# Transposing queries and keys of groups 1 to 3 by DMA instead of by TensorE, in sigmoid attention followed by an MLP mixer

## The chip, the cores and the metric

The kernel runs on one core of a Trainium2 chip. A core has TensorE (PE; its weight loads are shown as PEld), VectorE (DVE), ScalarE (ACT), GpSimd (POOL) and SyncE (SP), which each work through a queue of their own in order and wait for one another by semaphores, and 16 DMA engines, which serve the transfers that SP and POOL issue. The metric is the device time of one execution in microseconds (us); lower is better. Names such as `tk_1_2591` are the program's tiles; the last number is a running number of the buffer.

## What is computed

Eight batches, twelve heads, sequence 448, head dimension 64. Attention with a sigmoid in place of the softmax, then a mixer over tokens and one over channels:

```python
scores = scale * np.matmul(q, k.transpose(0, 1, 3, 2)) - np.log(S)
attn = 1.0 / (1.0 + np.exp(-scores))
attn_out = np.matmul(attn, v)                      # (8, 12, 448, 64)
x = attn_out.transpose(0, 2, 1, 3).reshape(B, S, H * D)   # (8, 448, 768)
xt = x.transpose(0, 2, 1)
h = np.maximum(xt @ w_tok1, 0.0) @ w_tok2          # 448 -> 256 -> 448 over tokens
u = x + h.transpose(0, 2, 1)
h2 = np.maximum(u @ w_ch1, 0.0) @ w_ch2            # 768 -> 1536 -> 768 over channels
return u + h2
```

## The kernel before

The batches go in four groups g of two (`b`), and the twelve heads of a group in six pairs i. A token is numbered 7p + j (p below 64, j below 7), so that the 128 partitions of a tile hold the 64 p of both batches, and j runs along the free dimension.

*Loading* (`load`, L75 and L83). The queries and keys of a pair come as float32 tiles `rawq`, `rawk` by two DMAs each on the SP queue, and are cast to float16 tiles `q`, `k` of [128, J, 2, 64], by VectorE for the very first pair and by GpSimd for all others. The values `v` are cast by the DMA itself, on POOL's queue. There are four raw buffers, three of `q` and three of `k`, six of `v`: a load waits for a cast to have read its raw buffer, a cast for its `q` or `k` buffer to be read.

*A pair of attention* (`attention_atoms`). `turn(i)` transposes `k` and `q` to have the head dimension on the partitions: for each of the two, seven 128x128 transposes on TensorE (L131), one for each j, into a PSUM bank, and a VectorE copy to `kT` (L135) or `qT` (L137); the copy of `qT` also reorders it so that a batch's 448 tokens lie together. `scores(i, j)` makes a tile of scores `qk` by four matmuls of 64x448 (L147), and ScalarE's sigmoid turns it to `attn` (L154). `values(i)` multiplies by `v` (L168), `back(i)` transposes the result to `x_nat` (L187, L190).

*The mixer of a group* (`mixer_atoms`). `tok1` (L222) and ScalarE's relu (L230) make `h1T`; `tok2` (L240) is added to `x_nat` by VectorE to give `u` (L247), cast (L252) and transposed (`uturn`, L257 and L262) to `uT`; `ch1` (L267, L274) makes `h2aT`; `ch2` (L286, L294) adds to `u`, and SP stores it (L297), two DMAs for each j.

*Order.* TensorE's instructions stand in the order in which they are written (`manual_schedule`). Group 0's attention stands alone; after that, `weave` puts the attention of group g+1 between the pieces of group g's mixer by a table of weights; the last mixer stands alone. The other queues are ordered by the scheduler, from the instructions' dependences and buffers. Eight PSUM banks serve: two tiles of two banks for scores, and four single banks (`bank`) shared in turn by all else, the transposes too.

Of the kernel before, what the change touches and what calls it, by code (L numbers as in the profile page):

```python
# [9 lines left out]
FP16 = mybir.dt.float16  # L10
# [9 lines left out]
def kernel(  # L20
# [13 lines left out]
    nc = tc.nc  # L34
# [5 lines left out]
    J = 7  # L40
    P = S // J
# [12 lines left out]
    pa = ctx.enter_context(tc.tile_pool(name="pa", bufs=2))  # L54
# [10 lines left out]
    heads = {}  # L65
# [46 lines left out]
    def bank(name, shape, dtype=FP32):  # L112
        return pp.tile(shape, dtype, tag="m", bufs=4, name=name)
# [3 lines left out]
    def attention_atoms(g):  # L117

        qT, kT, attn, xT = {}, {}, {}, {}
        x_nat = pa.tile([128, J, D], FP16, tag="x_nat", bufs=2, name=f"x_nat_{g}")  # L120
        x_nats[g] = x_nat

        def turn(i):
            kt = pa.tile([128, J, 2, P], FP16, tag="kT", bufs=2, name=f"kT_{g}_{i}")
            qt = pa.tile([128, 2, J, P], FP16, tag="qT", bufs=2, name=f"qT_{g}_{i}")
            kT[i], qT[i] = kt, qt
            for what in ("k", "q"):
                ps = bank(f"t{what}_{g}_{i}", [128, J, 2, P], FP16)
                src = heads[(g, i, what)]
                for j in range(J):  # L130
                    nc.tensor.transpose(  # L131
                        out=ps[:, j, :, :], in_=src[:, j, :, :], identity=ident[:, :]
                    )
                if what == "k":
                    nc.vector.tensor_copy(out=kt[:, :, :, :], in_=ps[:, :, :, :])  # L135
                else:
                    nc.vector.tensor_copy(  # L137
                        out=qt.rearrange("e b j p -> e j b p"), in_=ps[:, :, :, :]
                    )

        def scores(i, j):
            ps = pp.tile([128, 2, 512], FP32, tag="qk", bufs=2, name=f"qk_{g}_{i}_{j}")
            at = pa.tile([128, 2, S], FP16, tag="attn", bufs=11, name=f"attn_{g}_{i}_{j}")
            attn[(i, j)] = at
            for b in range(2):
                for h in range(2):
                    nc.tensor.matmul(  # L147
                        out=ps[64 * b : 64 * b + 64, h, 0:S],
                        lhsT=kT[i][64 * h : 64 * h + 64, j, b, :],
                        rhs=qT[i][64 * h : 64 * h + 64, b, :, :],  # L150
                        start=True,
                        stop=True,
                    )
            nc.scalar.activation(  # L154
                out=at[:, :, :],
                in_=ps[:, :, 0:S],
                func=SIGMOID,
                bias=bias_t[:, :],
                scale=att_scale,
            )  # L160

        def values(i):
            ps = [bank(f"xa_{g}_{i}_{b}", [128, S]) for b in range(2)]
            vf = heads[(g, i, "v")]
            for j in range(J):
                for h in range(2):
                    for b in range(2):
                        nc.tensor.matmul(  # L168
                            out=ps[b][64 * h : 64 * h + 64, :],
                            lhsT=vf[64 * b : 64 * b + 64, h, j, :],  # L170
                            rhs=attn[(i, j)][64 * b : 64 * b + 64, h, :],
                            start=(j == 0),
                            stop=(j == J - 1),
                        )
            xt = pa.tile([128, J, 2, P], FP16, tag="xT", bufs=2, name=f"xT_{g}_{i}")
            xT[i] = xt
            for b in range(2):
                nc.scalar.activation(
                    out=xt[:, :, b, :],
                    in_=ps[b].rearrange("d (j p) -> d j p", j=J),  # L180
                    func=COPYF,
                )

        def back(i):
            ps = bank(f"xb_{g}_{i}", [128, J, 128], FP16)
            for j in range(J):
                nc.tensor.transpose(  # L187
                    out=ps[:, j, :], in_=xT[i][:, j, :, :], identity=ident[:, :]
                )
            nc.vector.tensor_copy(  # L190
                out=x_nat[:, :, 128 * i : 128 * i + 128], in_=ps[:, :, :]
            )

        atoms = []
        nv = NP * J // 2
        for n in range(nv):

            def visit(n=n):
                for r in (2 * n, 2 * n + 1):
                    scores(r // J, r % J)  # L200

            atoms.append((float(n), 0.45, visit))
        for i in range(NP):
            atoms.append((i * J / 2 - 1.4, 0.8, lambda i=i: turn(i)))
            last = (i * J + J - 1) // 2
            atoms.append((last + 1.01, 1.4, lambda i=i: values(i)))
            atoms.append((last + 1.9, 0.4, lambda i=i: back(i)))
        return sorted(atoms, key=lambda a: a[0])
# [183 lines left out]
```

## Time and profile before

| | us |
|---|---|
| three runs | 433.65, 439.6, 435.13 |
| their median | 435.13 |
| the profiled execution | 434.62 |
| its span, first to last instruction | 432.8 |
| mean granted TensorE clock | 0.994 |

The times of single instructions below come from the profiled execution alone, whose span is 1.8 us shorter than its time. Loading and group 0's attention take the first 67 us of it, with the DMA engines busy nearly throughout; the three woven stretches, each of some 97 us, follow; the last mixer begins near 362 us. A line of the time view gives start, length, engine, source line, operation, the tile written and the tiles read, and in brackets what ended the idle time before it. A line of the stretch view gives the stretch, its length, for PE, PEld, DVE, ACT and POOL the busy time (and instructions), the granted clock, the busy share of the DMA engines and their GB/s. A line of the DMA view ends with the size of each transfer and the median time from issue to landing.

### The profile page before, as it was taken

What the parts mean: (1) busy time and instruction counts of PE and PEld (TensorE: products, weight loads), DVE (VectorE), ACT (ScalarE), POOL (GpSimd) and SP (SyncE); (2) the same over time, 40 slices, a digit from 0 to 9 for tenths busy, and PEclk for the clock granted to TensorE, in tenths of its full rate; (3) what the DMA queues carried; (4) which work ended last, traced back from release to release, by engine and by line L of the source; (5) the groups of instructions that cost most, each with busy time, mean ns of one, the idle gap of its engine ahead of it and who ended that gap; (6) DMA issues with size and microseconds to landing.
All of it is one profiled execution on the core that took longest, in us unless ns stands there. A gap on an engine that the chain in (4) does not pass through costs nothing.

```text
span 432.8 us, 8713 instructions
## 1 busy us (share of the span) xinstructions
PE 396.2 (92%) x3712; PEld 215.7 (50%) x3712; DVE 174.8 (40%) x312; ACT 216.8 (50%) x277; POOL 74.5 (17%) x105
## 2 busy tenths in 40 slices
PE   1775668999999999999999999999999999999995
PEld 1343335444555555444565555444555555546663
DVE  2131213845542224844542224844542224855322
ACT  1768884774546643775546643765546643300000
POOL 3851516021221211021221211011000000000000
PEclk9999989999999999999999999999999999999999
DMA  8999999335237643234337643200002221000234
GB/s 202 246 261 248 259 266 216 85 87 108 60 69 180 161 92 69 77 88 105 67 63 180 163 93 73 71 2 2 2 2 74 73 74 38 2 0 2 54 94 109
DMA packets 28023, 44.51 MB, mean 103 GB/s; under 512 B 3280, under 2 KB 23504, under 8 KB 27984
## 3 DMA queue, kind: packets, MB, share of 16 engines
q1 hardware_dynamic: 18304, 33.04, 28.6%
q0 software_dynamic: 9680, 10.92, 15.4%
q8 instruction: 29, 0.48, 0.5%
q14 instruction: 10, 0.08, 0.1%
HBM read 43.84 MB, written 11.01 MB: 127 GB/s over the span
## 4 chain that ended last, share of the span: by engine, by line
PE 85%; ACT 7%; issue 3%; DVE 2%; DMA 1%; SPq 0%; ACTq 0%; DVEq 0%
DMA rawq_0_76<-in_q_dram 1%; PE xa_5_0_787 L168 1%; PE xa_0_0_273 L168 1%; PE c_2_5_1_4890 L286 0%; PE c_2_4_1_4846 L286 0%; PE c_2_4_0_4809 L286 0%; PE c_2_3_1_4746 L286 0%; PE c_2_2_0_4654 L286 0%; PE c_2_1_1_4615 L286 0%; PE c_2_0_0_4490 L286 0%; PE c_1_6_0_3556 L286 0%; PE c_1_5_1_3507 L286 0%; PE c_1_4_1_3463 L286 0%; PE c_1_4_0_3426 L286 0%; PE c_1_3_1_3363 L286 0%
## 5 line engine op out<-in xcount | busy, mean ns | idle before, releaser
L267 PEld LDWEIGHTS <-w_ch_t 128*128 128x128 f16 x576 | 53.4, 98 | 53.8 <-issue 9.7
L286 PEld LDWEIGHTS <-h2aT_4980 128*128 128x128 f16 x168 | 16.4, 98 | 10.9
L286 PEld LDWEIGHTS <-h2aT_3597 128*128 128x128 f16 x168 | 15.6, 98 | 12.5 <-issue 3.2
L286 PEld LDWEIGHTS <-h2aT_2214 128*128 128x128 f16 x168 | 15.6, 98 | 12.5 <-issue 3.2
L286 PEld LDWEIGHTS <-h2aT_831 128*128 128x128 f16 x168 | 15.6, 98 | 12.5 <-issue 3.2
L240 PEld LDWEIGHTS <-w_tok_n 128*64 128x64 f16 x224 | 12.1, 108 | 9.0 <-issue 4.8
L222 PEld LDWEIGHTS <-w_tok_t 64*128 64x128 f16 x224 | 10.6, 94 | 7.8 <-issue 1.0
L131 PE MATMUL tk_0_165<-ident,k_0_74 128*128 128x128 f16 x7 | 0.9, 311 | 7.3 <-DVE k_0_74 L83 7.3
L154 ACT ACTIVATE attn_0_0_184<-qk_0_0_183,att_bias 128x896 f16<-128x896 f32 x1 | 1.0, 1007 | 10.1 <-PE qk_0_0_183 L147 10.1
L131 PEld LDWEIGHTS <-k_0_74 128*128 128x128 f16 x7 | 0.7, 141 | 7.3 <-DVE k_0_74 L83 7.3
L99 DVE COPY w_tok_n<-w_tok_s 128x896 f16<-128x896 f16 x1 | 1.6, 1562 | 5.5 <-DMA w_tok_s<-in_moe_w_tok_dram 5.5
L147 PEld LDWEIGHTS <-kT_0_163 64*64 64x64 f16 x28 | 1.1, 129 | 4.7 <-issue 4.5
L190 DVE COPY x_nat_162<-xb_5_820 128x896 f16<-128x896 f16 x1 | 0.6, 625 | 6.6 <-PE xb_5_820 L187 6.6
L83 DVE CAST k_0_74<-rawk_0_71 128x896 f16<-128x896 f32 x1 | 1.1, 1086 | 5.3 <-DMA rawk_0_71<-in_k_dram 5.3
L83 POOL CAST k_5_3738<-rawk_5_3735 128x896 f16<-128x896 f32 x1 | 0.9, 933 | 12.4 <-issue 12.4
L147 PEld LDWEIGHTS <-kT_2_329 64*64 64x64 f16 x28 | 0.9, 104 | 4.3 <-issue 3.5
L83 POOL CAST k_4_3725<-rawk_4_3722 128x896 f16<-128x896 f32 x1 | 0.9, 934 | 12.4 <-issue 12.4
L83 POOL CAST k_4_959<-rawk_4_956 128x896 f16<-128x896 f32 x1 | 0.9, 933 | 12.4 <-issue 12.4
L83 POOL CAST k_4_2342<-rawk_4_2339 128x896 f16<-128x896 f32 x1 | 0.9, 933 | 12.4 <-issue 12.4
L135 DVE COPY kT_1_225<-tk_1_227 128x896 f16<-128x896 f16 x1 | 0.6, 624 | 5.9 <-PE tk_1_227 L131 5.9
L147 PEld LDWEIGHTS <-kT_5_669 64*64 64x64 f16 x28 | 0.9, 106 | 4.3 <-issue 3.3
L75 POOL DMA_DIRECT2D v_3_953<-in_v_dram x2 | 1.2, 593 | 10.2 <-DMA w_ch_t<-in_moe_w_ch_dram 10.2
(1646 smaller groups left out, 1126.6 us busy)
## 6 DMA issues: line engine op xcount, KB each, us to landing
w_ch_t<-in_moe_w_ch_dram POOLq DMA_DIRECT2D x2, 2304.0 KB, 29.3
rawk_0_71<-in_k_dram SPq DMA_DIRECT2D x2, 224.0 KB, 4.0
rawq_0_76<-in_q_dram SPq DMA_DIRECT2D x2, 224.0 KB, 5.6
rawk_1_89<-in_k_dram SPq DMA_DIRECT2D x2, 224.0 KB, 7.3
rawq_1_94<-in_q_dram SPq DMA_DIRECT2D x2, 224.0 KB, 7.8
rawk_2_102<-in_k_dram SPq DMA_DIRECT2D x2, 224.0 KB, 7.1
rawq_2_107<-in_q_dram SPq DMA_DIRECT2D x2, 224.0 KB, 6.3
rawk_3_119<-in_k_dram SPq DMA_DIRECT2D x2, 224.0 KB, 7.2
```

The source lines that it names most:

```text
L75: eng.dma_start(out=t[64 * b : 64 * b + 64, :, :, :], in_=src[2 * g + b, 2 * i : 2 * i + 2].rearrange("h (p j) e -> p h j e", j=J),)
L83: eng.tensor_copy(out=t[:, :, :, :], in_=raw.rearrange("p h j e -> p j h e"))
L99: nc.vector.tensor_copy(out=w_tok2_n[:, :, :, :], in_=w_tok2_s.rearrange("t c (p j) -> t c j p", j=J),)
L131: nc.tensor.transpose(out=ps[:, j, :, :], in_=src[:, j, :, :], identity=ident[:, :])
L135: nc.vector.tensor_copy(out=kt[:, :, :, :], in_=ps[:, :, :, :])
L147: nc.tensor.matmul(out=ps[64 * b : 64 * b + 64, h, 0:S], lhsT=kT[i][64 * h : 64 * h + 64, j, b, :], rhs=qT[i][64 * h : 64 * h + 64, b, :, ...
L154: nc.scalar.activation(out=at[:, :, :], in_=ps[:, :, 0:S], func=SIGMOID, bias=bias_t[:, :], scale=att_scale,)
L168: nc.tensor.matmul(out=ps[b][64 * h : 64 * h + 64, :], lhsT=vf[64 * b : 64 * b + 64, h, j, :], rhs=attn[(i, j)][64 * b : 64 * b + 64, h, : ...
L222: nc.tensor.matmul(out=ps[b][:, :], lhsT=w_tok1_t[64 * b : 64 * b + 64, j, 128 * tcb : 128 * tcb + 128], rhs=x_nat[64 * b : 64 * b + 64, j ...
L240: nc.tensor.matmul(out=ps[64 * b : 64 * b + 64, :], lhsT=w_tok2_n[:, tcb, j, :], rhs=h1T[:, b, tcb, c], start=(tcb == 0), stop=(tcb == 1),)
L267: nc.tensor.matmul(out=ps[:, :, :], lhsT=w_ch1_t[:, db, 128 * cb : 128 * cb + 128], rhs=uT[:, db, j0:j1, :], start=(db == 0), stop=(db == ...
L286: nc.tensor.matmul(out=ps[:, :], lhsT=h2aT[:, cb, j, :], rhs=w_ch2_t[:, cb, c], start=(cb == 0), stop=(cb == NCB - 1),)
```

## The change

For groups 1 to 3, `turn` issues a transposing DMA from the `k` or `q` tile in SBUF straight to `kT` or `qT` in SBUF, on the SP queue, in place of seven transposes on TensorE, a PSUM bank and a copy. Group 0 keeps TensorE. `qT` takes the layout of `kT`, [128, J, 2, P] in place of [128, 2, J, P], in all groups, so its reader in `scores` takes seven runs of 64 elements that are 128 apart, where it took 448 in a row. Both get three buffers in place of two.

```diff
         def turn(i):
-            kt = pa.tile([128, J, 2, P], FP16, tag="kT", bufs=2, name=f"kT_{g}_{i}")
-            qt = pa.tile([128, 2, J, P], FP16, tag="qT", bufs=2, name=f"qT_{g}_{i}")
-            kT[i], qT[i] = kt, qt
-            for what in ("k", "q"):
+            for what, turned in (("k", kT), ("q", qT)):
+                t = pa.tile(
+                    [128, J, 2, P], FP16, tag=f"{what}T", bufs=3, name=f"{what}T_{g}_{i}"
+                )
+                turned[i] = t
+                src = heads[(g, i, what)]
+                if g > 0:
+                    nc.sync.dma_start_transpose(
+                        out=t.rearrange("e j b p -> e j (b p)"),
+                        in_=src.rearrange("p j h e -> p (j h e)"),
+                    )
+                    continue
                 ps = bank(f"t{what}_{g}_{i}", [128, J, 2, P], FP16)
-                src = heads[(g, i, what)]
                 for j in range(J):
                     nc.tensor.transpose(
                         out=ps[:, j, :, :], in_=src[:, j, :, :], identity=ident[:, :]
                     )
-                if what == "k":
-                    nc.vector.tensor_copy(out=kt[:, :, :, :], in_=ps[:, :, :, :])
-                else:
-                    nc.vector.tensor_copy(
-                        out=qt.rearrange("e b j p -> e j b p"), in_=ps[:, :, :, :]
-                    )
+                nc.vector.tensor_copy(out=t[:, :, :, :], in_=ps[:, :, :, :])
...
-                        rhs=qT[i][64 * h : 64 * h + 64, b, :, :],
+                        rhs=qT[i][64 * h : 64 * h + 64, :, b, :],
```

On TensorE, in the first third of group 2's woven stretch, this is the queue before, from the last scores ahead of pair 1's turn to the transposes of `u` behind it (each pair of rows is a weight load and its matmul; of each run of equal rows one is shown):

```order
L147 LDWEIGHTS kT_0_2366
L147 MATMUL qk_0_5_2582<-qT_0_2367,kT_0_2366 64x448
L131 LDWEIGHTS k_1_2303
L131 MATMUL tk_1_2591<-ident,k_1_2303 128x128
...
L131 LDWEIGHTS q_1_2308
L131 MATMUL tq_1_2600<-ident,q_1_2308 128x128
...
L257 LDWEIGHTS u_1_5_2512
L257 MATMUL ut_5_2609<-ident,u_1_5_2512 128x128
```

And this is the same place now (line numbers are two higher behind the edit):

```order
L149 LDWEIGHTS kT_0_2270
L149 MATMUL qk_0_5_2470<-qT_0_2272,kT_0_2270 64x448
L259 LDWEIGHTS u_1_5_2400
L259 MATMUL ut_5_2481<-ident,u_1_5_2400 128x128
...
L269 LDWEIGHTS w_ch_t
L269 MATMUL c_1_2_0_2489<-uT_2117,w_ch_t 128x512
```

The 14 transposes of the turn are gone, and the neighbours have closed up; nothing else has changed places there.

On SP, in the loading phase, these are the loads of group 1's last pairs before (in brackets the counts waited for: DMAHW is the completion of an earlier transfer on SP, Pool a cast):

```order
L75 DMA rawq_3_948<-in_q_dram 64x2x448 [waits DMAHW7_49,DMAHW6_49,Pool_49]
L75 DMA rawq_3_948<-in_q_dram 64x2x448
L75 DMA rawk_4_956<-in_k_dram 64x2x448 [waits DMAHW1_49,DMAHW0_49,Pool_49]
L75 DMA rawk_4_956<-in_k_dram 64x2x448
L75 DMA rawq_4_961<-in_q_dram 64x2x448 [waits DMAHW3_49,DMAHW2_49,Pool_49]
```

And now, where the transposes of group 1's pair 0 stand between them, and those of pairs 1 and 2 behind the group's last load:

```order
L75 DMA rawq_3_948<-in_q_dram 64x2x448
L131 DMA_TRANSPOSE kT_0_983<-k_0_907 128x7x128 [waits DMAHW0_49,DVE_49,PE_49]
L131 DMA_TRANSPOSE qT_0_985<-q_0_912 128x7x128 [waits DMAHW1_49,DVE_49]
L75 DMA rawk_4_956<-in_k_dram 64x2x448 [waits DMAHW2_49,Pool_49]
...
L75 DMA rawq_5_974<-in_q_dram 64x2x448 [waits DMAHW1_49]
L131 DMA_TRANSPOSE kT_1_1190<-k_1_920 128x7x128 [waits DMAHW2_49,DVE_49,PE_49]
L131 DMA_TRANSPOSE qT_1_1192<-q_1_925 128x7x128 [waits DMAHW3_49,DVE_49]
L131 DMA_TRANSPOSE kT_2_1350<-k_2_933 128x7x128 [waits DMAHW4_49,DVE_49,PE_49]
L131 DMA_TRANSPOSE qT_2_1352<-q_2_938 128x7x128 [waits DMAHW5_49,DVE_49]
L75 DMA rawk_0_2191<-in_k_dram 64x2x448 [waits DMAHW6_49,Pool_49]
```

The wait for PE is for the scores of the pair three before, which free the buffer of `kT`.

On SP, near the end of group 1's woven stretch, the transposes of group 2's first two pairs stand between the stores of group 0's `u`:

```order
L299 DMA out_dram<-u_0_987 64x768 [waits DMAHW1_49]
L131 DMA_TRANSPOSE kT_0_2270<-k_0_2194 128x7x128 [waits DMAHW2_49,PE_49]
L131 DMA_TRANSPOSE qT_0_2272<-q_0_2199 128x7x128 [waits DMAHW3_49]
...
L299 DMA out_dram<-u_2_1017 64x768 [waits DMAHW3_49]
L131 DMA_TRANSPOSE kT_1_2477<-k_1_2207 128x7x128 [waits DMAHW4_49,PE_49]
L131 DMA_TRANSPOSE qT_1_2479<-q_1_2212 128x7x128 [waits DMAHW5_49]
L299 DMA out_dram<-u_3_1040 64x768 [waits DMAHW6_49,DVE_49]
```

Before, this queue held only loads and stores there; a store of `u` that stands behind a transpose is issued after it.

## The prediction

> **What bounds the kernel now.** I read the page's busy times first, then the busy times by stretch, then the instructions in order of time around the transposes, and at last the DMA queues. The page's first lines and its chain:
>
> ```profile
> span 432.8 us, 8713 instructions
> PE 396.2 (92%) x3712; PEld 215.7 (50%) x3712; DVE 174.8 (40%) x312; ACT 216.8 (50%) x277; POOL 74.5 (17%) x105
> ...
> PE 85%; ACT 7%; issue 3%; DVE 2%; DMA 1%; SPq 0%; ACTq 0%; DVEq 0%
> ```
>
> TensorE is busy for 92% and carries 85% of the chain that ended last. An average hides stages, so the stretch in which groups 1 to 3 are computed is looked at alone (columns: stretch, its length, then busy time of each engine, granted clock, busy share of the DMA engines, GB/s):
>
> ```profile
> 70.00:267.00 197.00, 195.33 (x1893) 105.61 (x1890) 84.95 (x154) 109.86 (x143) 36.96 (x50) 1.00 0.46 106
> 190.00:275.00 85.00, 84.45 (x829) 46.13 (x828) 35.11 (x65) 44.80 (x59) 16.21 (x22) 1.00 0.47 107
> ```
>
> TensorE is busy 84.45 of 85 us at the full clock; ScalarE has 44.80 and VectorE 35.11. What is taken off TensorE's queue here shortens the span one for one, until another wait takes its place. The DMA engines are half idle (0.46).
>
> **What the change removes.** One turn is 14 transposes and two VectorE copies. In steady state (start, length, engine, line):
>
> ```profile
> 183.64 0.56 PE L131 MATMUL tk_1_2591<-ident,k_1_2303 128*128 128x128 f16 x7
> 184.04 0.55 PE L131 MATMUL tq_1_2600<-ident,q_1_2308 128*128 128x128 f16 x7
> 184.25 0.62 DVE L135 COPY kT_1_2589<-tk_1_2591 128x896 f16<-128x896 f16 x1 [0.31 <-PE tk_1_2591 L131]
> 184.43 0.50 PE L257 MATMUL ut_5_2609<-ident,u_1_5_2512 128*128 128x128 f16 x6
> 187.67 0.36 PE L147 MATMUL qk_1_0_2640<-qT_1_2590,kT_1_2589 64*64 64x448 f16 x4
> ...
> 197.91 0.56 PE L131 MATMUL tk_2_2767<-ident,k_2_2316 128*128 128x128 f16 x7
> ```
>
> The turn holds TensorE from 183.64 to 184.43, when the next work starts: 0.79 us. Its copies end well before the scores at 187.67, so no wait of TensorE goes with them. Turns of pairs 1 to 5 of three groups: 15 x 0.79 = 11.85 us.
>
> The first turn of a group stands between the last token-mixing matmul and the next work, and there it hides something:
>
> ```profile
> 169.46 0.56 PE L131 MATMUL tk_0_2368<-ident,k_0_2290 128*128 128x128 f16 x7
> 169.95 0.48 ACT L230 ACTIVATE h1T_2212<-k_1_1_1_1_2270 128x384 f16<-128x384 f32 x1
> 170.34 0.52 PE L240 MATMUL yn_0_0_2387<-h1T_2212,w_tok_n 128*64 128x384 f16 x4
> 170.60 0.61 DVE L137 COPY qT_0_2367<-tq_0_2377 128x896 f16<-128x896 f16 x1
> 170.69 0.49 PE L240 MATMUL yn_0_1_2393<-h1T_2212,w_tok_n 128*64 128x384 f16 x4
> 171.13 0.54 DVE L247 TENSOR_TENSOR u_0_2386<-x_nat_982,yn_0_0_2387 128x384 f32<-128x384 f16 x1
> 171.60 0.54 DVE L247 TENSOR_TENSOR u_0_2386<-x_nat_982,yn_0_1_2393 128x384 f32<-128x384 f16 x1
> ```
>
> It takes 0.88 us (169.46 to 170.34). Without it yn_0_0 can start at 169.46, but yn_0_1 needs the second half of h1T, written until 170.43. VectorE paces this place. Its second addition can start when yn_0_1 is done, near 170.45 + 0.49 + about 0.15 (an estimate from 170.34 + 0.52 to the start at 171.13, which was held by the copy), so about 171.1 for 171.60: a gain near 0.45 instead of 0.88. The wait that becomes late next is h1T's. Three times 0.45 is 1.35 us; bounds are 0 and 0.88 each. Sum removed: 11.85 + 1.35 = 13.2 us. The 36 copies (36 x 0.62 = 22 us of VectorE) and 36 uses of a PSUM bank cost nothing elsewhere: TensorE idles 0.55 us in 85, so beyond the 13.2 at most about 3 x 0.55 = 1.6 us can come of them.
>
> **What it adds.** 36 transposing DMAs on SP, each moving 128 x 896 two-byte elements, 224 KB. No row shows such a DMA. The nearest rows are loads and stores on the same queue:
>
> ```profile
> q1 hardware_dynamic: 18304, 33.04, 28.6%
> ...
> rawk_3_2326<-in_k_dram SPq DMA_DIRECT2D x2, 224.0 KB, 3.5
> ...
> 213.00:219.00 6.00, 6.00 (x60) 3.19 (x61) 3.21 (x6) 2.45 (x3) 1.09 (x2) 1.00 0.55 154
> 331.00:336.00 5.00, 5.00 (x41) 2.79 (x38) 1.64 (x3) 1.90 (x2) 0.00 (x0) 1.00 0.33 82
> ```
>
> *By bytes*: 33.04 MB took 28.6% of 432.8 us on all engines, 123.8 us, so 267 GB/s, and 229,376 bytes take 0.86 us. *By packets*: 123.8 x 16 / 18304 is 0.108 us a packet; a block of 128 columns is 256 bytes of a row, so a transpose has 7 x 128 = 896 pieces, and 896 x 0.108 / 16 = 6.05 us. The two stretches decide between the ends. In the first, loads in pieces of 1792 bytes (7 x 64 x 4) moved 924 KB in 0.55 x 6 x 16 = 52.8 engine-us, 102 ns a piece; in the second, stores in pieces of 3072 bytes moved 410 KB in 26.4, 198 ns a piece. Time goes with bytes, and no fixed part per piece shows. So I take the low end, doubled for the transposing to about 2 us of all sixteen engines, and a landing near the 3.5 us of a load; 0.86 and 6.05 stay as bounds.
>
> The Trainium skill (DMA: Bandwidth & Descriptors, Latency and other measured facts) gives 261 GB/s for a transposing DMA with a non-contiguous middle dimension, by which one would be an estimated 0.88 us and the sum would stand. The Trainium skill (VectorE: DVE Perf Modes, The three transpose paths) speaks against the change: 390 ns for a 128x128 block on TensorE and 1309 ns through the DMA crossbar; seven in a row would be an estimated 9.2 us. The trace has TensorE at 0.79 us for 14 blocks, 56 ns each, and no run here shows the other side.
>
> Cover: two full pairs. With three buffers of kT a transpose waits for the scores of the pair three before, so it may be issued some two pairs (2 x 14.3 us, from 183.64 to 197.91) before its own scores. Behind it on SP stand loads for the next casts and stores of u; these wait at most for scores already in progress. Its casts are as far ahead: on POOL k and q of pair 3 and later now wait for a DMA's read instead of a transpose on TensorE, and the v loads queued behind them wait with them; both lie a pair ahead of use. So 36 x 2 us in the half-idle DMA engines, and SP's issue time (0.6 us for a plain one), are put at nothing. If landings passed 20 us, this cover would be gone.
>
> The tight place is group 1's first pair, in the loading phase:
>
> ```profile
> 55.53 1.25 SPq L75 DMA_DIRECT2D rawq_3_948<-in_q_dram  x2
> 78.75 0.38 PE L147 MATMUL qk_0_0_1094<-qT_0_984,kT_0_983 64*64 64x448 f16 x4
> ...
> 57.00:72.00 15.00, 11.16 (x144) 6.36 (x145) 1.25 (x2) 10.07 (x17) 4.70 (x7) 0.89 1.14 243
> ...
> rawk_1_917<-in_k_dram SPq DMA_DIRECT2D x2, 224.0 KB, 15.9
> ...
> rawk_3_943<-in_k_dram SPq DMA_DIRECT2D x2, 224.0 KB, 10.9
> ```
>
> The two transposes are issued right behind rawq_3, at about 57, into full DMA engines (1.14); a load took 10.9 us there. Together they land near 69 to 72; the scores want them at about 78.3. No cost, with 6 us to spare.
>
> qT now has its rows of 64 elements 128 apart, so the moving operand of the scores is strided, in group 0 too. No row shows a strided moving read; bounds are 0 and a doubled time:
>
> ```profile
> 179.94 0.38 PE L147 MATMUL qk_0_2_2545<-qT_0_2367,kT_0_2366 64*64 64x448 f16 x4
> 180.15 0.36 PE L147 MATMUL qk_0_3_2552<-qT_0_2367,kT_0_2366 64*64 64x448 f16 x4
> ```
>
> A tile of scores takes 0.21 us of TensorE; doubled, 126 tiles would add 26.5 us. Runs of 64 elements are long, so I take 0.
>
> **Sum.** The profiled execution took 434.62 us (span 432.8); the median shown is 435.13, 0.5 above. 434.62 - 13.2 = 421.4 us.
>
> **Rivals.** (1) *Late first pair, within 2%.* If the two transposes follow one another at the 10.9 to 15.9 us of that phase's loads, qT lands at 57 + 21.8 to 57 + 31.8, so 79 to 89, against 78.3: a stall of up to 10.5 us once, and 421.4 + 5 to 421.4 + 10.5, say 430. For it: the full engines; against: their load falls away at 72. (2) *DMA becomes the bound, slower.* From 70 to 267 us the engines are free for 0.54 x 197 = 106 us, and 28 transposes (five pairs of group 1, six of group 2, three of group 3) must pass. They fit up to 106 / 28 = 3.8 us each. At 6.05 us they need 169 us: 63 us more than there is, and only the last six turns or so keep their gain (6 x 0.79 = 4.7): 434.6 + 63 - 4.7 = 493 us. It is slower by 2% from about 4.3 us each. For it: 0.108 us a packet; against: the two stretches above. By the Trainium skill's 1309 ns (VectorE: DVE Perf Modes, The three transpose paths) it would be an estimated 28 x 9.2 = 258 us, and 582 us in all. (3) *Strided scores, slower*: 421.4 + 26.5 = 448 us.
>
> **Chances and numbers.** Hidden, as forecast: 0.61. Late first pair or like stalls of 5 us and more: 0.16. DMA bound: 0.18. Strided scores: 0.05. Two per cent (8.7 us) is about what a measurement of this kernel can tell from no change. Faster by more than that needs less than 426.4: 0.61; within: 0.16; slower: 0.18 + 0.05 = 0.23. The forecast's own range is 418.5 (13.2, 1.3 more if the first turns count in full, and the 1.6: 16.1 us) to 426. The range for 8 in 10 leaves out the DMA bound alone and reaches over the strided case: 418.5 to 450.
>
> **What would show it.** Right: no transposes of q and k on TensorE after group 0, turn to turn 0.8 us shorter, 13 us less busy TensorE, transposes landing in under 10 us, no wait of L149 for a DMA. Wrong: TensorE idle before the first scores of a pair with kT or qT as releaser (once near 78 us: rival 1; at every pair, with a DMA share near 1: rival 2); a score tile over 0.21 us, in group 0 too: rival 3. One thing would undo the argument: a transpose that holds the SP queue or the rings so long that loads and stores behind it come late.

## The result, and the profile after

| | before | after |
|---|---|---|
| median (lowest to highest), 4 runs each | 436.88 (433.65 to 439.6) | 424.08 (423.59 to 425.05) |
| the profiled execution | 434.62 | 423.59 |
| its span | 432.8 | 421.8 |

The changed kernel takes 0.9713 of the time (95% interval 0.9634 to 0.9791), 12.8 us less by the medians. Ratios leave out the executions that lie more than 1.5% above the fastest of their kernel, and medians and ranges do not, so a ratio is not always the quotient of the medians shown. The forecast was faster, 421.4 us, with 418.5 to 426 for itself; the kind came out as forecast, and so did the size of the gain (13.2 us).

First the page of the changed kernel:

```profile
span 421.8 us, 8216 instructions
...
PE 385.5 (91%) x3460; PEld 202.9 (48%) x3460; DVE 155.7 (37%) x276; ACT 216.9 (51%) x277; POOL 74.4 (18%) x105
...
q1 hardware_dynamic: 51712, 41.30, 43.2%
...
PE 84%; ACT 8%; issue 3%; DVE 2%; DMA 1%; SPq 0%; ACTq 0%; DVEq 0%
```

TensorE is still the bound, with 252 instructions fewer (18 turns of 14). Queue q1 now carries 51712 packets for 18304: 33408 more, 928 for each of the 36 transposes. It holds the sixteen engines for 0.432 x 421.8 = 182.2 us instead of 123.8, which is 58.4 / 36 = 1.62 us for one transpose.

The stretch view, cut where a group's first token-mixing matmul starts (columns as before). Of the kernel before:

```profile
164.80:262.00 97.20, 96.37 (x931) 52.06 (x932) 42.47 (x77) 53.92 (x69) 18.02 (x24) 1.00 0.43 101
...
53.00:66.00 13.00, 8.59 (x113) 4.57 (x112) 1.78 (x3) 10.62 (x13) 1.60 (x3) 0.87 1.13 263
```

And of the changed kernel:

```profile
69.80:162.80 93.00, 91.78 (x848) 47.53 (x846) 36.54 (x65) 53.97 (x69) 25.92 (x35) 1.00 0.94 184
162.80:255.30 92.50, 91.74 (x847) 47.49 (x846) 36.00 (x65) 53.97 (x69) 17.77 (x24) 1.00 0.62 123
255.30:347.80 92.50, 91.74 (x847) 47.51 (x846) 36.00 (x65) 53.97 (x69) 0.00 (x0) 1.00 0.21 47
53.00:66.00 13.00, 9.93 (x93) 5.22 (x93) 1.87 (x3) 8.81 (x12) 2.29 (x3) 0.50 1.13 265
```

A woven stretch is 92.50 us instead of 97.2, and TensorE's busy time falls by as much (96.37 to 91.74). The time came out of TensorE's queue, while the DMA share rose from 0.43 to 0.62 in the second stretch. In the first it stands at 0.94; what room is left there is the question of e3 and e4. (The share can come out a little above 1.) The last row of each shows another thing: the granted clock in group 0's attention was 0.50 in this execution and 0.87 in that of before.

Cut in this way, the two profiled executions and those of the experiments read as follows (us; "group 0" is the time up to the first token-mixing matmul, "rest" what follows the third woven stretch, which is the last mixer):

| kernel | group 0 | woven 1 | woven 2 | woven 3 | rest | span |
|---|---|---|---|---|---|---|
| before | 67.65 | 97.15 | 97.16 | 97.15 | 73.69 | 432.8 |
| after | 69.83 | 92.97 | 92.50 | 92.50 | 74.00 | 421.8 |
| e10, after once more | 71.86 | 92.49 | 92.50 | 92.49 | 73.96 | 423.3 |
| e1, TensorE keeps all turns | 70.36 | 97.16 | 97.15 | 97.15 | 73.78 | 435.6 |
| e2, groups 2 and 3 alone | 72.80 | 97.15 | 92.50 | 92.50 | 73.75 | 428.7 |
| e7, turned by both | 71.55 | 97.11 | 96.94 | 96.94 | 73.96 | 436.5 |
| e3, every DMA twice | 72.58 | 95.04 | 92.94 | 92.50 | 74.24 | 427.3 |
| e4, every DMA three times | 67.02 | 117.51 | 110.36 | 92.85 | 73.96 | 461.7 |
| e8, two buffers | 71.42 | 92.84 | 92.50 | 92.50 | 74.34 | 423.6 |
| e8, one buffer | 75.20 | 118.64 | 118.78 | 193.38 with the rest | | 506.0 |
| e5, group 0 too | 116.47 | 92.50 | 92.49 | 92.50 | 73.74 | 467.7 |
| e6, `back` too | 71.82 | 90.34 | 90.35 | 90.35 | 74.04 | 416.9 |
| e11, e6 once more | 72.19 | 90.35 | 90.34 | 90.35 | 73.97 | 417.2 |
| e9, e6 and `uturn` of groups 1, 2 | 70.04 | 91.91 | 92.43 | 91.83 | 74.19 | 420.4 |

The woven stretches of groups 2 and 3 repeat to 0.01 us where nothing stalls. Group 1's does so less well (92.97 and 92.49 for the same kernel; the last section has the reason), and group 0 does not repeat at all. So what an edit does in a woven stretch can be read to a few hundredths from one trace, while a median carries group 0's wandering.

The place named as tight, group 1's first pair, in the changed kernel's time view (SP issues) and, below, the last fields of its DMA view (us from issue to landing):

```profile
58.31 1.31 SPq L131 DMA_TRANSPOSE kT_0_983<-k_0_907  x1
59.72 8.87 SPq L131 DMA_TRANSPOSE qT_0_985<-q_0_912  x1
69.02 1.26 SPq L75 DMA_DIRECT2D rawk_4_956<-in_k_dram  x2
```

```profile
kT_0_983<-k_0_907 SPq DMA_TRANSPOSE x1, 15.6
qT_0_985<-q_0_912 SPq DMA_TRANSPOSE x1, 16.7
kT_1_1190<-k_1_920 SPq DMA_TRANSPOSE x1, 10.2
qT_1_1192<-q_1_925 SPq DMA_TRANSPOSE x1, 11.1
...
qT_5_4428<-q_5_3551 SPq DMA_TRANSPOSE x1, 2.9
```

The first transpose of `q` lands at 59.72 + 16.7 = 76.4, and while the engines are full its issue alone holds SP for 8.87 us. The scores that read it:

```profile
80.64 0.38 PE L149 MATMUL qk_0_0_1078<-qT_0_985,kT_0_983 64*64 64x448 f16 x4
80.86 0.36 PE L149 MATMUL qk_0_1_1085<-qT_0_985,kT_0_983 64*64 64x448 f16 x4
```

They start with 4.2 us to spare, and two tiles of scores are 0.22 us apart, as before (179.94 to 180.15): the strided read costs nothing. From group 2 on, a transpose lands 2.9 to 5.8 us after its issue, and 2.9 to 3.0 at the end of group 3, where it has the engines to itself.

### The profile page after: what moved, and what is told of

Its sections match the earlier page's. It is cut to its first block, busy times and chain, and to the rows that moved or that the text cites. A ratio compares the mean times of both kernels' runs of the same rounds, so it can differ in the third digit from the quotient of the medians.

```text
span 421.8 us, 8216 instructions
## 1 busy us (share of the span) xinstructions
PE 385.5 (91%) x3460; PEld 202.9 (48%) x3460; DVE 155.7 (37%) x276; ACT 216.9 (51%) x277; POOL 74.4 (18%) x105
## 3 DMA queue, kind: packets, MB, share of 16 engines
q1 hardware_dynamic: 51712, 41.30, 43.2%
## 4 chain that ended last, share of the span: by engine, by line
PE 84%; ACT 8%; issue 3%; DVE 2%; DMA 1%; SPq 0%; ACTq 0%; DVEq 0%
DMA rawq_0_76<-in_q_dram 1%; PE xa_0_0_273 L170 1%; PE xa_4_0_717 L170 1%; PE xa_5_0_787 L170 1%; PE c_2_6_0_4651 L288 0%; PE c_2_5_1_4602 L288 0%; PE c_2_4_1_4558 L288 0%; PE c_2_4_0_4521 L288 0%; PE c_2_3_1_4458 L288 0%; PE c_2_2_0_4382 L288 0%; PE c_2_1_1_4343 L288 0%; PE c_2_1_0_4282 L288 0%; PE c_1_5_1_3315 L288 0%; PE c_1_4_1_3271 L288 0%; PE c_1_4_0_3234 L288 0%
## 5 line engine op out<-in xcount | busy, mean ns | idle before, releaser
L288 PEld LDWEIGHTS <-h2aT_3405 128*128 128x128 f16 x168 | 15.6, 98 | 13.0 <-issue 3.6
L288 PEld LDWEIGHTS <-h2aT_831 128*128 128x128 f16 x168 | 15.6, 98 | 13.0 <-issue 3.6
L288 PEld LDWEIGHTS <-h2aT_2118 128*128 128x128 f16 x168 | 15.6, 98 | 13.0 <-issue 3.6
L288 PEld LDWEIGHTS <-h2aT_4692 128*128 128x128 f16 x168 | 16.4, 98 | 10.9
L156 ACT ACTIVATE attn_0_0_184<-qk_0_0_183,att_bias 128x896 f16<-128x896 f32 x1 | 1.0, 1007 | 10.2 <-PE qk_0_0_183 L149 10.2
L83 POOL CAST k_0_3481<-rawk_0_3478 128x896 f16<-128x896 f32 x1 | 0.9, 936 | 25.7 <-issue 25.7
L83 POOL CAST k_3_3520<-rawk_3_3517 128x896 f16<-128x896 f32 x1 | 0.9, 935 | 11.5 <-DMA kT_0_3557<-k_0_3481 11.5
L232 ACT ACTIVATE h1T_2116<-k_1_0_0_0_2119 128x384 f16<-128x384 f32 x1 | 0.5, 491 | 4.7 <-PE k_1_0_0_1_2120 L224 4.7
L232 ACT ACTIVATE h1T_4690<-k_3_0_0_0_4693 128x384 f16<-128x384 f32 x1 | 0.5, 491 | 4.7 <-PE k_3_0_0_1_4694 L224 4.7
L232 ACT ACTIVATE h1T_3403<-k_2_0_0_0_3406 128x384 f16<-128x384 f32 x1 | 0.5, 491 | 4.7 <-PE k_2_0_0_1_3407 L224 4.7
```

Of the source, the lines that this page charges most:

```text
L83: eng.tensor_copy(out=t[:, :, :, :], in_=raw.rearrange("p h j e -> p j h e"))
L232: nc.scalar.activation(out=h1T[:, b, tcb, c], in_=ps[b][:, :], func=RELU)
L288: nc.tensor.matmul(out=ps[:, :], lhsT=h2aT[:, cb, j, :], rhs=w_ch2_t[:, cb, c], start=(cb == 0), stop=(cb == NCB - 1),)
```

## The experiments

Each is an edit of the changed kernel, with the kernel before run beside it on the same chip. Three sets were run: e1, e2, e3 and e7 (before: 438.28 us, median of 19); e4, both e8 and e6 (435.46, of 7); e10, e11, e5 and e9 (439.06, of 7).

**e1: the layout and the buffers alone.** TensorE keeps the turns of all groups; `qT` has its new layout, and both tiles their three buffers.

```diff
-                if g > 0:
+                if False:
```

> All groups keep TensorE for the transposes; only the layout of qT (strided moving operand of the scores) and the third buffers are left of the change. Theory A (the gain is TensorE's time in the 18 turns and nothing else): the time of before, ratio 0.995 to 1.005, woven groups 97.1 us apart as before, a score tile 0.21 us. Rival B (layout and buffers cost something in group 0, which would explain the 2.2 us that group 0 lost in the profile of the changed kernel): 1 to 3 us slower than before, with the loss ahead of the first token-mixing matmul. Rival of the strided read: 450 us or more.

Measured: 439.86 us (437.35 to 441.52), ratio 1.0103 (0.9999 to 1.0206). The woven stretches are those of before, 97.15 to 97.16 us. So neither the strided read of `qT` nor the third buffer costs or gains anything there: the third rival is out. Whether the layout or the buffers cost 1 to 3 us in group 0 is settled neither by this ratio nor by the one trace (70.36 us); the part on the sum comes back to it.

**e2: groups 2 and 3 alone.**

```diff
-                if g > 0:
+                if g > 1:
```

> Only groups 2 and 3 are transposed by DMA; group 1, whose first transposes run in the loading phase, keeps TensorE. Theory A: two of three woven groups gain 4.65 us, so 9.3 us off before, ratio near 0.979, about 4.4 us more than the changed kernel. Rival B' (the early transposes of group 1 delay group 0 by about 2 us): 9.3 us off as well, but the changed kernel is then only some 2 us better than this one, and group 0 ends as early as before.

Measured: 427.85 us (424.13 to 431.96), ratio 0.9803 (0.9644 to 0.9962). The first stretch is again 97.15 us, the others 92.50: each group brings its own 4.65 us, with no help from the others.

**e7: turned by both.** The transposing DMAs as changed, and TensorE's 14 transposes too, into a bank of PSUM that nothing reads; only VectorE's copies are left out.

```diff
                         in_=src.rearrange("p j h e -> p (j h e)"),
                     )
-                    continue
...
-                nc.vector.tensor_copy(out=t[:, :, :, :], in_=ps[:, :, :, :])
+                if g == 0:
+                    nc.vector.tensor_copy(out=t[:, :, :, :], in_=ps[:, :, :, :])
```

> Groups 1 to 3 are transposed by DMA as in the changed kernel, and TensorE transposes them too, into a PSUM bank that nothing reads; the 36 VectorE copies stay away. Theory A (the gain is TensorE's queue time): 15 x 0.79 + 3 x about 0.45 us come back, 434 to 437 us, ratio to before 0.995 to 1.005. Rival C (the gain is relief of VectorE and of the waits on its copies): the time stays near the changed kernel's 424 us.

Measured: 438.1 us (434.87 to 440.99, 10 runs), ratio 1.0036 (0.9984 to 1.0087). Its second woven stretch, in the stretch view:

```profile
168.66:265.60 96.94, 96.10 (x929) 51.95 (x929) 35.93 (x65) 53.97 (x69) 17.94 (x24) 1.00 0.64 128
```

VectorE is at 35.93 us as in the changed kernel and the DMA share at 0.64, but TensorE is back at 96.10, and the stretch lasts 96.94. Put beside 97.16 and 92.50, this splits the gain: about 0.2 us of 4.66 comes of the copies, all else of TensorE's queue (its busy time rises by 4.36 us, the stretch by 4.44).

**e3 and e4: every transposing DMA twice, and three times.** The extra ones read the same source and write spare tiles that nothing reads (`range(1)` in e3, `range(2)` in e4).

```diff
+                    for r in range(2):
+                        x = pa.tile([128, J, 128], FP16, tag="spare", bufs=4, name=f"x{what}_{g}_{i}_{r}")
+                        nc.sync.dma_start_transpose(
+                            out=x[:, :, :],
+                            in_=src.rearrange("p j h e -> p (j h e)"),
+                        )
                     continue
```

> Each transposing DMA is followed by a second one of the same source into a spare tile that nothing reads, so the DMA engines do twice the transposing. From the packets' share a transpose costs 1.6 us of all sixteen engines; 28 of them twice are 91 us, where 106 us were free. Theory A (cover holds up to 3.8 us each): the time of the changed kernel within 1.5%, 422 to 430 us, a stall at most in group 1. Rival (the DMA side is already what paces the kernel, the cover is thin): 28 x 1.6 = 45 us more, 465 us or more.

> Each transposing DMA of groups 1 to 3 is followed by two more of the same source into spare tiles that nothing reads: three times the transposing. Theory A' (the DMA engines are the cover, and it ends where 28 transposes of T us each fill the 106 us that were free): 28 x 3 x 1.6 = 136 us do not fit, 30 us too much, so 445 to 460 us, DMA share near 1 through the woven stretches of groups 1 and 2, and TensorE waiting for kT or qT there; group 3's stretch, which has no loads, stays at 92.5 us. Rival (single transfers overlap so well that the engines' busy share is no limit): within 1% of the doubled one, 427 to 435 us.

e3 measured 430.7 us (429.12 to 435.05, 10 runs), ratio 0.9884 (0.9841 to 0.9927), a little above what was expected; e4 462.97 us (2 runs), ratio 1.0621 (1.0517 to 1.0725), above it too. Stretches and waits of e3, the waits as engine, line, releaser, total us, times, longest:

```profile
72.58:167.62 95.04, 91.73 (x847) 47.50 (x846) 36.58 (x65) 53.97 (x69) 20.44 (x27) 1.00 1.04 190
167.62:260.56 92.94, 91.64 (x845) 47.67 (x845) 36.09 (x65) 53.97 (x69) 20.18 (x28) 1.00 1.00 182
```

```profile
PE qk L155 <- DMA qT<-q: 2.5, 1, 2.5
```

The two issues on SP that this wait goes back to:

```profile
72.00 1.64 SPq L131 DMA_TRANSPOSE kT<-k  x1
...
79.74 1.26 SPq L131 DMA_TRANSPOSE qT<-q  x1
```

Stretches of e4, and then its waits on TensorE and on VectorE:

```profile
70.00:180.00 110.00, 89.26 (x779) 44.69 (x775) 35.08 (x62) 51.89 (x64) 17.18 (x23) 0.91 1.03 180
180.00:285.00 105.00, 89.87 (x796) 46.09 (x789) 34.86 (x63) 52.12 (x67) 20.45 (x28) 0.90 0.98 186
```

```profile
PE qk L155 <- DMA qT<-q: 20.4, 3, 9.7
PE yn L248 <- DVE u L255: 14.7, 2, 7.4
```

```profile
DVE u L255 <- DMA out_dram<-u: 19.1, 4, 7.7
```

With twice the transposes the DMA engines are full through two stretches (1.04 and 1.00), and all it costs there is one stall of 2.5 us at group 1's first scores and some tenths, 3.0 us in all. (The ten runs lie at 429.12 us and above, the eight of the changed kernel at 425.44 and below, and the medians are over 6 us apart. The part of this that the woven stretches do not show was not traced.) With three times the two stretches are 25 and 18 us longer. The engine time is 235.0 us in e3 (0.550 x 427.3) and 284.4 in e4 (0.616 x 461.7), so an extra transpose takes 1.47 and 1.42 us, and what stands in place of one turned tensor is 3.1 and 4.5 us. The working had put the limit at 3.8, and the two lie on either side of it. That fits a lack of room in the engines, but does not prove it, since the extra transposes load SP's queue too. By the time view SP is issuing for about 102 of the 117.5 us of e4's first stretch and 81 of the 95 of e3's (59 of 93 in the changed kernel), and it puts extra transposes ahead of real ones: e3's first `kT` and `qT` are issued at 72.00 and 79.74, where the changed kernel issued them at 58.31 and 59.72. So the stall of 2.5 us comes of a late issue too. In e4 scores wait for `qT`, and VectorE waits for stores of `u` that SP issues late, behind transposes, and that free the buffers it writes. In these stretches the granted clock is 0.91 and 0.90.

**e8: two buffers, and one, of `kT` and `qT` in groups 1 to 3** (group 0 keeps three under a tag of its own). The edit is shown with one; the other has 2 in its place.

```diff
-                    [128, J, 2, P], FP16, tag=f"{what}T", bufs=3, name=f"{what}T_{g}_{i}"
+                    [128, J, 2, P], FP16, tag=f"{what}T{min(g, 1)}", bufs=3 if g == 0 else 1, name=f"{what}T_{g}_{i}"
```

> kT and qT have two buffers in groups 1 to 3, so a transpose can be issued one pair ahead of its scores and not two. Theory A (a landing of 3 to 6 us is covered by one pair of some 14 us): as the changed kernel, 422 to 428 us, woven groups 92.5 us apart. Rival (two pairs of cover are needed, since SP's queue is in order and loads and stores stand between): a stall in each pair, 430 us or more.

> kT and qT have one buffer in groups 1 to 3, so a transpose is issued only when the last scores of the pair before are done, and its own scores stand right behind those on TensorE. Theory A (the latency is there and only the cover hides it): each of the pairs 1 to 5 of three groups stalls for the issue of the first (1.3 us) and the landing of the second (3.0 us), 15 x 4.3 to 4.6 = 65 to 69 us more, 487 to 495 us. Rival (latency hardly matters): under 440 us.

Two buffers: 426.48 us (2 runs), ratio 0.9784 (0.9684 to 0.9883), and stretches of 92.84, 92.50 and 92.50, with no wait of TensorE for a transpose: one pair of cover is enough. One buffer: 507.77 us (one run), more than expected. Its waits:

```profile
PE qk L149 <- DMA qT<-q: 55.2, 15, 4.5
```

Fifteen waits of 3.7 us: the landing of a lone transpose with its issue, now in the open, since a transpose may start only when the scores of the pair ahead are done. That is 55.2 / 3 = 18.4 us a group, while a stretch is 26.2 us longer than in the changed kernel. The other 7.8 are in TensorE's busy time, 99.51 and 99.53 us in the first two stretches instead of 91.7. The time view shows where:

```profile
219.83 0.59 PE L149 MATMUL qk<-qT,kT 64*64 64x448 f16 x4 [4.49 <-DMA qT<-q]
220.96 4.46 PE L269 MATMUL c<-uT,w_ch_t 128*128 128x512 f16 x12
...
234.17 2.76 PE L269 MATMUL c<-uT,w_ch_t 128*128 128x512 f16 x12
```

After a wait of 4.49 us the next 12 matmuls take 4.46 us, and 13 us later the same number takes 2.76. The stretch view of this place has the reason in its granted clock (the number behind the busy times):

```profile
219.80:221.00 1.20, 1.17 (x11) 0.82 (x12) 0.00 (x0) 0.48 (x1) 0.94 (x1) 0.50 0.07 14
...
223.00:224.00 1.00, 1.00 (x4) 0.35 (x3) 0.23 (x1) 0.00 (x0) 0.00 (x0) 0.50 0.52 108
...
225.00:226.00 1.00, 1.00 (x18) 0.43 (x20) 0.54 (x1) 0.15 (x1) 0.00 (x0) 1.00 0.24 56
```

It is 0.50 for more than 4 us after the wait, and 1.00 from 225 on: the stall is paid for once more, in the clock.

**e5: group 0 too.**

```diff
-                if g > 0:
+                if True:
```

> Group 0 is transposed by DMA too. Theory A (a DMA transpose pays only where its landing is covered and the DMA engines have room; in the loading phase neither holds, and its first pair stands on SP behind the loads of pairs 1 to 4): the first scores come 10 to 20 us later than 11 us, 434 to 444 us in all, the woven groups still 92.5 us apart. Rival (TensorE paces group 0 as well): 420 us or less.

Measured: 468.65 us (2 runs), ratio 1.0665 (1.0588 to 1.0742), far above what was expected. The woven stretches are untouched (92.49 to 92.50); the whole loss is group 0, 116.47 us instead of 69.83. In the time view, SP and then TensorE's first scores:

```profile
20.94 3.25 SPq L131 DMA_TRANSPOSE kT<-k  x1
24.23 10.58 SPq L131 DMA_TRANSPOSE qT<-q  x1
34.85 2.92 SPq L131 DMA_TRANSPOSE kT<-k  x1
37.81 16.74 SPq L131 DMA_TRANSPOSE qT<-q  x1
...
60.54 1.25 SPq L75 DMA_DIRECT2D rawk<-in_k_dram  x2
```

```profile
51.07 0.96 PE L149 MATMUL qk<-qT,kT 64*64 64x448 f16 x8 [51.07 <-DMA qT<-q]
```

TensorE does nothing until 51.07 (11.76 in the changed kernel). The first pair's transposes stand on SP behind ten loads of two DMAs each, and go into engines that are full (a DMA share of 1.22 from 20 to 40 us); the longest landing of a `qT`, that of the first pair, is 26.8 us, and from 20.94 to 60.54 SP issues six transposes and not one load, so the later pairs come late as well.

**e6: the way back too.** On top of the change, `back` of pairs 0 to 4 in groups 1 to 3 is done by DMA; pair 5 keeps TensorE, since the mixer wants its result at once.

```diff
+            if g > 0 and i < NP - 1:
+                nc.sync.dma_start_transpose(
+                    out=x_nat[:, :, 128 * i : 128 * i + 128],
+                    in_=xT[i].rearrange("d j b p -> d (j b p)"),
+                )
+                return
```

> On top of the change, the transposes of attention's result back to tokens (back) for pairs 0 to 4 of groups 1 to 3 are made by transposing DMAs on SP too. Theory A (what leaves TensorE's queue in a woven stretch shortens it one for one while the landing is covered): 15 x 0.40 us, 6.0 us better than the changed kernel, near 418 us, woven groups 90.5 us apart. Rival (15 more entries in SP's queue that wait for ScalarE hold up loads, stores and the transposes behind them): no gain or a loss, 424 us or more.

Measured: 418.04 us (417.34 to 419.03, 4 runs), ratio 0.9585 (0.9511 to 0.9658). Its stretches, the first with a DMA share of 1.00 and yet no wait of TensorE for a transpose:

```profile
71.82:162.16 90.34, 89.61 (x811) 45.27 (x809) 33.40 (x60) 53.91 (x69) 22.59 (x30) 1.00 1.00 186
162.16:252.51 90.35, 89.63 (x810) 45.30 (x810) 33.33 (x60) 53.91 (x69) 20.75 (x28) 1.00 0.74 149
```

Another 2.15 us a group, 0.43 for each seven transposes, by the same rule: an instruction taken off TensorE's queue shortens the stretch by its time on it.

**e10 and e11: the changed kernel and e6 again, side by side.**

> The changed kernel once more, beside the others of this job. Theory A (what the change gains is the woven stretches' 13.5 us and nothing in group 0, whose length differs from run to run): 0.965 to 0.975 of before, woven groups 92.5 us apart. Rival (its group 0 is systematically longer): its first token-mixing matmul later than 70 us again, and less than 12 us gained.

> The changed kernel with back of pairs 0 to 4 of groups 1 to 3 on transposing DMAs, once more: 3 x 2.16 = 6.5 us better than the changed kernel of the same job, woven groups 90.3 us apart. Rival (the 6 us of the job before came from differences between runs): within 3 us of the changed kernel.

Measured: 424.49 us (423.01 to 425.44), ratio 0.9657 (0.9608 to 0.9706), and 419.22 us (418.79 to 422.76), ratio 0.9563 (0.9495 to 0.9631). e6 is 5.3 us below the change by the medians; the stretches say 6.4 (277.48 to 271.04). It is the fastest version found. The changed kernel's first token-mixing matmul comes at 71.86 us again, but by the medians it gains 14.6 us here and not less than 12, so that rival does not stand.

**e9: e6, and `uturn` of groups 1 and 2 by DMA.**

```diff
+            if g in (1, 2):
+                nc.sync.dma_start_transpose(out=uT[:, :, j, :], in_=u16s[j][:, :])
+                return
```

> On top of back by DMA, the transposes of u (uturn) of the mixers of groups 1 and 2 are made by DMA too, which takes 7 x 0.34 us off TensorE and 7 x 0.81 us off ScalarE in each. Theory A (where the result is wanted at once, the landing of 3 to 4.5 us shows): ch1 starts 2 us or so later than before in both groups, woven groups 2 and 3 are 90 to 93 us apart, so no gain, 417 to 423 us. Rival (only TensorE's queue counts): 2.4 us less in each of the two, 87.9 us apart.

Measured: 422.14 us (2 runs), ratio 0.9607 (0.954 to 0.9674), 2.9 us above e11. The stretches that hold these turns are 2.1 and 1.5 us longer than e6's, although TensorE has less to do. SP's issues in the second stretch, and the waits of TensorE for `uT` in the whole span:

```profile
169.54 11.41 SPq L264 DMA_TRANSPOSE uT<-u  x7
```

```profile
PE c L278 <- DMA uT<-u: 5.2, 2, 3.1
```

The seven transposes of `u` are issued one by one behind VectorE's casts, from 169.54 to 180.95, and `ch1` wants them at once. TensorE waits 3.1 us in one group and 2.1 in the other, while its busy time falls by 1.6 and 1.2 only (from 89.63 and 89.62 in e6 to 88.06 and 88.37). The first stretch, which has none of these turns, is 1.57 us longer too: 0.8 of it is a wait for the `qT` of group 1's second pair, and some 0.5 may be a cast of VectorE's that takes 1.10 us instead of 0.55 (last section); the rest is not accounted for.

## Why the prediction was right

- **The bound, and 15 turns of 0.79 us.** Right. TensorE's queue pays one for one (e7), group by group (e2), also for other transposes (e6). The woven stretches give 4.65 us a group, 3.95 of which are five turns of 0.79.
- **The first turns, 0.45 us each.** Under-sized: 4.65 - 3.95 = 0.70 us. The time view of the changed kernel at the same place, group 2:

```profile
162.80 0.33 PE L224 MATMUL k_1_0_0_0_2119<-x_nat_982,w_tok_t 64*128 64x384 f16 x1
...
167.80 1.00 PE L242 MATMUL yn_0_1_2281<-h1T_2116,w_tok_n 128*64 128x384 f16 x4
167.94 0.48 ACT L232 ACTIVATE h1T_2116<-k_1_1_1_1_2174 128x384 f16<-128x384 f32 x1
...
168.84 0.56 DVE L249 TENSOR_TENSOR u_0_2274<-x_nat_982,yn_0_1_2281 128x384 f32<-128x384 f16 x1 [0.27 <-PE yn_0_1_2281 L242]
```

  The working let yn_0_1 start only when the second half of h1T is written. It starts at 167.80, before that half is begun, and spreads over 1.00 us: only its end waits for h1T. VectorE's second addition comes 6.04 us behind the group's first matmul, where the working had 6.3 and the kernel before 6.80 (164.80 to 171.60).
- **36 copies and PSUM banks at nothing.** Right within 0.2 us a group (e7, which leaves the copies out and keeps the banks in use).
- **The price of a transposing DMA.** Taken as 2 us of the sixteen engines between 0.86 and 6.05; it is 1.62 on average, and 1.42 to 1.47 for each extra one of e3 and e4. The 1.62 us are 28 ns of one engine for each of 928 packets, so time did not go with the number of pieces at the loads' 108 ns. The Trainium skill (VectorE: DVE Perf Modes, The three transpose paths) has 1309 ns for one 128x128 block; seven blocks here land in 3.0 us together, and the 9.2 us of that rival does not stand. Its 261 GB/s (DMA: Bandwidth & Descriptors, Latency and other measured facts) gave an estimated 0.88 us; 229,376 bytes in 1.62 us are 142 GB/s, so that was too low by nearly half.
- **Room: break-even at 3.8 us.** Not contradicted: 3.1 us costs 3 us in the woven stretches (e3), 4.5 costs over 40 (e4). That too many transposes slow the kernel is shown, and by this limit the change stays clear by a factor of 2.3 in price. Whether the engines or SP's queue set the limit stays open, as said at e4, and a DMA share of 1.00 is no sign of it: e6 has that share and no wait.
- **Group 1's first pair, landing 69 to 72, 6 us spare.** Under-sized. The step took one load's 10.9 us for both; the transposes took 15.6 and 16.7, and `qT` landed at 76.4, with 4.2 us spare. Part of these 4.2 us is luck: the scores came at 80.64 and not near 78.3, since group 0 took 2.18 us longer in this execution. The first rival was that near: in e3, where the first `qT` is issued later, it does stall TensorE, for 2.5 us. SP was also held for 8.87 us there, which the 0.6 us of an issue did not allow for; TensorE waited for none of the loads behind it. Of the signs that the working named for being right, a landing in under 10 us failed at four transposes of group 1 (10.2 to 16.7).
- **The order on SP at nothing.** Right as changed. Transposes that wait on SP for buffers hold the stores and loads behind them for long, and TensorE does not feel it. The longest two of these waits in the changed kernel (the releaser is inferred; for the second of them, the scores that free `kT` end at 184.30 and the issue starts at 184.35):

```profile
SPq L131 <- PE ut_6_3806 L259: 20.3, 1, 20.3
SPq L131 <- PE ut_6_2519 L259: 20.2, 1, 20.2
```

  This has an end, as e4 shows with its late stores.
- **Cover of two pairs.** More than is needed: one pair does (e8 with two buffers). One buffer gives none, and there each of 15 pairs costs 3.7 us and the slower clock besides.
- **The strided read at nothing.** Right (e1).
- **The sum.** The woven stretches gave 291.46 - 277.97 = 13.49 us against 13.2: three larger first turns (+0.75) less 0.47 us in group 1, which is told below. The profiled times differ by only 11.0 us, since group 0 took 2.18 us more in the execution profiled after and the rest 0.31. Group 0's length is 67.0 to 75.2 us over all these traces but e5's. It is 70.36 in e1, which has no transposing DMA, and 72.80 in e2, which issues none before group 1's stretch; but both have the new layout and buffers. What the kernel before does by itself shows in its 28 executions that the experiments' ratios use: eight with a mean granted clock of 0.993 or 0.994 have spans of 431.4 to 433.7 us, eighteen with 0.967 to 0.979 have 434.1 to 437.4, and two with 0.964 have 439.3 and 439.9. With the woven stretches and the rest of its trace taken off, an estimated 66 to 75 us are left for group 0, half of them above 70.9; for the eight executions of the changed kernel the same estimate gives 70 to 72. So the 2.18 us are within what varies without the change, and the profile before was one of its short ones; a small part of the change's own is not excluded. The working tied its sum to one profiled execution near the fast end of this wandering (434.62, with medians of 435.46 to 439.06 in four sets); 13.2 below the median of 436.88 would have been 423.7.

## What to carry to other kernels

Where one engine is busy 99% of a stretch, an instruction taken off its queue is worth its spacing there, and a transpose can go to the DMA engines as long as its result is wanted a few microseconds after its source is ready and the engines have room: compare price times count with the idle DMA time of each stretch, not of the span, and the time of the issues with what the issuing queue has left. Leave transposes on TensorE where the consumer stands right behind (one buffer, `uturn`) or where the DMA queue is full of loads (group 0): there a transpose costs its landing, holds up the loads behind it, and the stall slows the matmuls after it. Where one early phase wanders by some microseconds from run to run, read an edit's worth from the stretches that repeat.

## What the runs showed of the hardware that was not expected

- *A transposing DMA holds its issuing queue.* Where the engines have room, SP needs 1.2 to 1.3 us to issue most of those of 128 x 896, twice a plain DMA's 0.6. In engines that are full with loads it took up to 8.87 us in the changed kernel and 16.74 in e5.
- *A stall costs twice.* A wait of 4.49 us is followed by matmuls at about 0.6 of their speed (4.46 us for 2.76), with a granted clock of 0.50 until at least 224 and 1.00 from 225 on (e8, one buffer). The Trainium skill (TensorE: Matmul & The Clock Gate, Part 1: The HAM clock gate) has the clock halved after an idle window of about 3.4 us, and restored after as long a busy one. The halving agrees with these rows; the clock came back later, between 4.2 and 5.2 us after the wait. Why the granted clock was 0.50 in group 0's attention, where TensorE's waits are near 1 us, no run tells.
- *VectorE beside GpSimd.* Group 1's stretch of the changed kernel is 0.47 us longer than the others. In its time view:

```profile
76.48 0.94 POOL L83 CAST q_3_951<-rawq_3_948 128x896 f16<-128x896 f32 x1 [1.53 <-DMA qT_0_985<-q_0_912]
...
76.80 1.02 DVE L254 CAST u_0_0_1000<-u_0_987 128x768 f16<-128x768 f32 x1
...
78.67 0.55 DVE L254 CAST u_0_1_1015<-u_1_1002 128x768 f16<-128x768 f32 x1
```

  GpSimd's cast, which now waits for the transposing DMA to have read its buffer, falls on VectorE's, and that takes 1.02 us instead of 0.55; the transposes of `u` on TensorE stand right behind. In e10, the same kernel, GpSimd's cast was over at 77.10, before VectorE's began at 78.83: the cast took 0.55 us and the stretch 92.49. Two more traces show the same: VectorE's cast takes 1.10 us in e9 (from 78.42, under a GpSimd cast that ends at 79.10) and 1.22 in e8 with two buffers (from 83.99, under one that ends at 84.79). In all three it ends 0.40 to 0.42 us after GpSimd's. The Trainium skill (SBUF — State Buffer, SBUF: two separate sides) says that the two share a pair of ports, and that for some of VectorE's instructions the one that starts first holds it for its whole instruction while the other stands still. The rows fit, but no run here was made to test it.
